# Letting ScalarE or VectorE take each cast and copy of the attention and folding stage, by the planner's estimates

## The chip, the cores and the metric

The kernel runs on one core of a Trainium2 chip. The engines named here are TensorE (PE, matrix products; PEld is its weight load), VectorE (DVE), ScalarE (ACT), GpSimd (POOL) and SyncE (SP), which only issues transfers. Each engine works through its own list in the order in which the instructions were recorded; an instruction whose input is not there holds up all that stand behind it in that list. The metric is the time of one execution in microseconds (us), the median over three runs.

## The reference

An attention over 4 batches x 12 heads, 448 tokens, head width 64, with soft-capped scores; then two feed-forward layers in a row.

```python
scores = cap * np.tanh(scale * q @ k.T / cap)
attn = np.exp(scores - max) / (sum + 1e-09)
x = attn @ v                       # 1792 x 768
x = ((x @ w1) * (x @ w2)) @ w3 @ w_out
h = x @ w_in
solu = h * softmax(h)
out = (layernorm(solu) * g_ln) @ w_out2
```

Between the product of the gates and `h` stand three matrices and no nonlinearity, so the kernel multiplies w3, w_out and w_in with each other first: these products of weights alone are the folds.

## The kernel before, in words

Every fp32 operand of a product is split into a high part, the operand cast to fp32r, and a low part, the operand less its high part; a product is then three matmuls (low by high, high by low, high by high). `cast` (L324) makes the high part on ACT, `low` (L327) the low part on DVE.

**The stages.** Stage one interleaves two streams on PE. One is attention: 24 pairs of heads, each with four blocks of scores (`scores`, L401, tiles `sc`, blocks 0 to 2 for two heads and block 3 for the rest of the keys of both), a tanh and an exp on ACT for each block (`exps`, L422: L426 and L431, tile `p`), and the product with the values and the sums (`values`, L480, tiles `o` and `n`, L486). The other, `beside` (L987), first folds w_out with w3 (`f1`, 576 matmuls, L658), then w_in with that (`f2`, 288 matmuls, L692), then begins the gated layer (`ab`, L935). When attention is done, stage two runs the rest of the gated layer, and stage three the last layers.

**Where the fold's operands come from.** A weight lands by DMA in one of three buffers `ld`, three DVE instructions turn it from 64-bit to 32-bit floats in one of two buffers `cv` (`convert`, L306: L314, L317, L320), then follow `cast` (L325) and `low` (L328). The operands are called `w_o` (w_out), `w_3` (w3), `w_i` (w_in), `wt` (the gates) and, loaded back from memory, `w34` (profile: w<-l). Attention's own are `qh`, `ql`, `kh`, `kl` from the loads `qd`, `kd` (`split_pair`, L375), and, for the gated layer, `xs` from `xr`.

**What sets the order.** Stage one is recorded by a planner, the class `Order` (L70). A step is a tuple: its engine, a rank, how long the engine is taken (`pitch`), when its result is there (`late`), and the instruction. `put` (L76) queues a step with the time at which its inputs are ready; `advance` (L103) takes, engine by engine, the step that can begin first by these estimates (then the lowest rank). The loop at L1073 decides for PE by the same clock: if the next piece of attention is ready it goes, otherwise one matmul of `beside` goes if its operands are ready, otherwise the clock moves on. So the estimates decide only the order; what happens on the chip is set by that order and the true durations. Before the change each step names one engine: casts and copies ACT, except the casts of pair 1 on DVE (L387; pair 0 is not split). After attention `order.live` is false, and steps are recorded at once in program order.

**Buffers that hold attention.** Scores use two places in PSUM, each taken from its first matmul until its exp has ended. Block 3 of a pair with an odd number therefore waits for the exp of block 2 of the pair before it.

Of the kernel before, what the change touches and what calls it, by code (L numbers as in the profile page):

```python
# [9 lines left out]
F32 = mybir.dt.float32  # L10
# [22 lines left out]
PLAIN, XR = 6, 5  # L33
# [36 lines left out]
class Order:  # L70
# [63 lines left out]
class Ahead:  # L134
# [20 lines left out]
    def step(self, n=1):  # L155

        for taken in range(n):
            if self.rest is not None:
                key, rest = self.rest
                for *_, do in rest():  # L160
                    do()
# [8 lines left out]
            for *_, do in first():  # L170
                do()
            self.rest = key, rest
            self.at += 1
            self.loads()
        return n
# [54 lines left out]
def attention_moe_solu(ctx: ExitStack, tc: tile.TileContext, q, k, v, cap, w12, w3t, wo, win, wout2, g_ln, out):  # L230
# [93 lines left out]
    def cast(th, x):  # L324
        act.copy(th, x)  # L325
# [8 lines left out]
    def plan64(key, src, n, dst, gate=None, there=None):  # L334

        i, slots, to = len(ahead.items), [], []

        def first():
            steps = convert(i, n, slots)
            return steps  # L340

        def begin():
            to.extend((*dst(), cvs.pop(i)))
            cast(to[0], to[2])

        def rest():
            return [("act", 1, 500, 680, begin), ("dve", 3, 610, 750, lambda: low(*to)), ("none", 0, 0, 0, lambda: ring["cv"].give(slots[0], order.now))]
# [27 lines left out]
    def split_pair(n, t):  # L375
# [5 lines left out]
        def make(name, w, x):  # L381
# [98 lines left out]
    def values(n):  # L480
# [21 lines left out]
        order.put(("act", 0, 460, 620, lambda: act.copy(to, out[:, :S])), order.now + 300, lambda t: ring["o"].give(slot, t))  # L502
        if n < PLAIN or m % 2 == 1:
# [22 lines left out]
            def keep():  # L526
# [3 lines left out]
                act.copy(copied[0], total[:, :S])  # L530
# [4 lines left out]
            order.put(("act", 0, 460, 620, keep), order.now + 300, kept)  # L535
# [80 lines left out]
    def load34(m):  # L616
# [12 lines left out]
        def high():  # L629
            t.append(ev_p.tile([P, 2, NC * P], F32R, tag="w34", bufs=2, name=f"w34_{f}_{nh}"))  # L630
            held_at["w34", m] = ring["w34"].take()
            cast(t[0][:, 0], ld[0])
# [6 lines left out]
        def landed(time):  # L639
            order.chain([("act", 1, 780, 920, high), ("dve", 1, 880, 1020, lambda: low(t[0][:, 0], t[0][:, 1], ld[0]))], time, finished, lambda: ring["w34"].when())  # L640
# [5 lines left out]
    def fold():  # L646
        for fq in range(NQ):
            for c in range(NC):
# [12 lines left out]
                def evict(f=f, fq=fq, c=c, slot=slot):  # L661
                    ev = []

                    def copy():
                        ev.append(ev_p.tile([P, HALF], F32, tag="ev", bufs=2, name=f"e1_{fq}_{c}"))
                        ev.append(ring["ev"].take())
                        act.copy(ev[0][:, :QW], f[:, :QW])
# [13 lines left out]
                    order.put(("act", 0, 310, 460, copy), order.now + 300, kept, lambda: ring["ev"].when())  # L681
                evict()
        for m_, (nh, f_) in enumerate(todo):
# [12 lines left out]
            def evict(f=f, f_=f_, nh=nh, slot=slot):  # L696
                ev = []

                def copy():
                    ev.append(ev_p.tile([P, HALF], F32, tag="ev", bufs=2, name=f"e2_{f_}_{nh}"))  # L700
                    ev.append(ring["ev"].take())
                    act.copy(ev[0], f)
# [4 lines left out]
                order.put(("act", 0, 510, 680, copy), order.now + 300, kept, lambda: ring["ev"].when())  # L707
# [52 lines left out]
    def plan_x(b, parts=range(NPAIR // 2)):  # L760
        for part in parts:
# [51 lines left out]
    def plan_sums(kind, dr, t_dr, i_, part, n):  # L813
# [12 lines left out]
        ahead.add((kind, i_, part), lambda: landing(i, four(dr, i_, part, n), 4 * n, F32), list, lambda: [(rest,)], None, lambda: 0.0 if "ts" in place else None)  # L826
# [26 lines left out]
    def plan_block(m, part):  # L853
        there = since((lambda: "ws" in place) if m != EARLY[4] else (lambda: (NF + 5, PASSES[1][1]) in fin and ("tg", NF // 2 - 1, 1) in ahead.done))
        ahead.add(("f", m, part), lambda: block_load(m, part, W4, tw_dr, fifth(m)), list,
                  lambda: [(lambda: block_split(ws[m], part),)], None, there)
# [62 lines left out]
    ahead.add("a0", load_first, list, lambda: [(first_operands,)], None, since(lambda: (NF + 2, PASSES[1][0]) in fin))  # L919

    def gated():
# [21 lines left out]
        def evict(f, b, i):  # L943
            bank_, slot = pp[f, b, i]

            def copy():
                pp["a", f, b] = place["ab"].tile([P, S], F32, tag="a", bufs=2, name=f"a_{f}_{b}")
                held_at["a", f, b] = ring["a"].take() if order.live else 0
                act.copy(pp["a", f, b], bank_[:, :S])  # L949
# [16 lines left out]
            if i == 0:  # L966
                order.put(("act", 0, 460, 620, copy), order.now + 300, lambda t: ring["f"].give(slot, t), lambda: ring["a"].when())
# [76 lines left out]
    with tc.manual_schedule():  # L1044
# [28 lines left out]
        for when, go in attend():  # L1073
            while True:
# [19 lines left out]
                assert waits[0] < 3e5, (order.now, pos, ask)  # L1094
# [348 lines left out]
```

## Time and profile before

| | us |
|---|---|
| median of three runs | 804.28 (803.32 to 804.76) |
| the profiled execution, its own time | 806.41 |
| its span in the trace | 804.6 |

Busy in the span: PE 785.3 us (98%), DVE 534.1 (66%), ACT 454.3 (56%), POOL 54.2 (7%). PE is the engine whose work cannot be taken away here, so its idle time and the time in which its clock is granted at half are what can be saved. Of the PE's time, matmuls at L935 take 233.8 us, at L486 78.6, at L658 76.3, at L692 68.3. The mean granted clock is 0.985 of full speed: it is 1.00 in most slices of the span and lower in the first eighth. The profile's rows read: line, engine, operation, out<-in, shape, count, then busy time and mean time of one, or in a view in order of time the start, the duration, and in brackets the idle time just before and what ended it.

### The profile page before, as it was taken

The numbers are of one execution on the slowest core, as the hardware profiler recorded it, in microseconds if no ns is written. First come the engines' busy times: TensorE is split into PE (matmuls) and PEld (weight loads), VectorE is DVE, ScalarE is ACT, GpSimd is POOL, SyncE is SP. The second block draws the span as 40 slices with busy tenths as digits, with TensorE's granted clock in tenths as the row PEclk, the third lists the DMA queues.
The fourth block names the chain that finished last, engine by engine and source line by source line (L and its number), as shares of the span: only waits on it lengthen the run. The fifth ranks groups of instructions, "written<-read, shape, count | busy, mean of one in ns | idle before, by whom it ended". The sixth has DMA issues, their size and how long they took to land.

```text
span 804.6 us, 11753 instructions
## 1 busy us (share of the span) xinstructions
PE 785.3 (98%) x4259; PEld 640.1 (80%) x4259; DVE 534.1 (66%) x938; ACT 454.3 (56%) x689; POOL 54.2 (7%) x106
## 2 busy tenths in 40 slices
PE   6989899999999999999999999999999999999998
PEld 3556668896776567766999999999788888899997
DVE  5466766678985356786678474332686668878972
ACT  5788766737868677766233221112476667845642
POOL 0101100100110011000000100000011111100000
PEclk8889999999999999999999999999999999999999
DMA  6475645487794349464898899982733335997431
GB/s 237 150 216 183 200 156 162 141 268 270 262 300 122 91 132 290 126 220 185 298 316 273 247 374 402 372 284 86 221 111 123 111 101 122 281 201 144 130 92 78
DMA packets 145705, 162.48 MB, mean 202 GB/s; under 512 B 66612, under 2 KB 116336, under 8 KB 144112
## 3 DMA queue, kind: packets, MB, share of 16 engines
q1 hardware_dynamic: 143056, 156.01, 60.6%
q0 software_dynamic: 2592, 5.73, 3.3%
q8 instruction: 33, 0.54, 0.3%
q14 instruction: 24, 0.20, 0.1%
HBM read 114.04 MB, written 47.53 MB: 201 GB/s over the span
## 4 chain that ended last, share of the span: by engine, by line
PE 89%; DMA 3%; ACT 3%; DVE 3%; issue 1%; SPq 0%; POOL 0%; DVEq 0%; ACTq 0%
PE ab L935 27%; PE u L1130 16%; PE f L658 9%; PE o L486 8%; PE f L692 8%; PE v L1130 8%; PE sc L413 6%; PE y L1130 4%; PE n L486 2%; PE sc L409 2%; ACT sc L426 1%; ACT p L431 1%; DMA wg<-wg_dr 1%; DMA rb<-r_dr 1%; DMA qd<-in_q 1%
## 5 line engine op out<-in xcount | busy, mean ns | idle before, releaser
L935 PE MATMUL ab<-xs,wt 128*128 128x448 f32 x1152 | 233.8, 363 | 0.0
L935 PEld LDWEIGHTS ab<-xs,wt 128*128 128x128 f32 x1152 | 215.5, 188 | 18.7 <-issue 4.5
L426 ACT ACTIVATE sc<-sc,small 128x896 f32<-128x896 f32 (+1 forms) x96 | 83.4, 892 | 51.5 <-PE sc L413 49.8
L431 ACT ACTIVATE p<-sc,small 128x896 f32<-128x896 f32 (+1 forms) x96 | 85.0, 921 | 0.4
L1130 PE MATMUL u<-ws,a 128*128 128x512 f32 x336 | 80.2, 390 | 0.3 <-DVE a L1258 0.3
L658 PEld LDWEIGHTS f<-w,w_o 128*128 128x128 f32 x576 | 72.8, 197 | 8.5 <-issue 4.1
L486 PE MATMUL o<-p,vd 128*64 128x448 f32 x384 | 78.6, 552 | 0.0
L658 PE MATMUL f<-w,w_o 128*128 128x256 f32 x576 | 76.3, 291 | 1.5 <-ACT w_o L325 0.6
L1130 PEld LDWEIGHTS u<-ws,a 128*128 128x128 f32 x336 | 63.0, 188 | 13.9 <-DVE a L1258 0.7
L692 PE MATMUL f<-w_i,w 128*128 128x512 f32 x288 | 68.3, 393 | 0.0
L692 PEld LDWEIGHTS f<-w_i,w 128*128 128x128 f32 x288 | 53.6, 188 | 13.9 <-issue 3.0
L1130 PE MATMUL u<-wg,a 128*128 128x384 f32 x336 | 62.1, 335 | 0.0
L486 PEld LDWEIGHTS o<-p,vd 128*64 128x64 f32 x384 | 25.7, 138 | 41.9 <-issue 41.9
L1130 PEld LDWEIGHTS u<-wg,a 128*128 128x128 f32 x336 | 58.6, 188 | 0.3 <-DVE a L1258 0.3
L949 ACT COPY a<-ab 128x448 f32<-128x448 f32 x32 | 16.9, 531 | 65.7 <-PE ab L935 57.8
L317 DVE SCALAR_TENSOR_TENSOR cv<-ld,cv 128x512 uint32<-128x512 uint32 (+1 forms) x80 | 51.5, 661 | 1.1
L320 DVE SCALAR_TENSOR_TENSOR cv<-ld,cv 128x512 uint32<-128x512 uint32 (+1 forms) x80 | 51.3, 660 | 0.8
L1254 ACT CAST a<-s 128x512 fp32r<-128x512 f32 (+1 forms) x42 | 31.3, 754 | 31.2 <-DVE s L1276 17.0
L314 DVE TENSOR_SCALAR cv<-ld 128x512 uint32<-128x512 uint32 (+1 forms) x80 | 32.0, 408 | 20.6 <-DMA ld<-in_w 8.3
L452 DVE TENSOR_TENSOR s<-p,p 128x896 f32<-128x896 f32 x18 | 19.7, 1092 | 34.0 <-ACT p L431 24.0
L1130 PE MATMUL v<-ws,a 128*128 128x512 f32 x168 | 40.4, 389 | 0.0
L1258 DVE TENSOR_TENSOR a<-s,a 128x512 fp32r<-128x512 f32 (+1 forms) x42 | 35.5, 851 | 5.8 <-ACT a L1254 5.8
(140 smaller groups left out, 1084.1 us busy)
## 6 DMA issues: line engine op xcount, KB each, us to landing
ld<-in_w SPq DMA_DIRECT2D x24, 512.0 KB, 5.0
w_dr<-wt SPq DMA_DIRECT2D x6, 1536.0 KB, 7.1
wt<-w_dr SPq DMA_DIRECT2D x6, 1536.0 KB, 8.6
ld<-in_w3t SPq DMA_DIRECT2D x16, 512.0 KB, 4.1
ab_dr<-abs SPq DMA_DIRECT2D x32, 224.0 KB, 4.1
ldx<-ab_dr SPq DMA_DIRECT2D x14, 512.0 KB, 4.4
c_dr<-h SPq DMA_DIRECT2D x14, 512.0 KB, 2.7
ldx<-c_dr SPq DMA_DIRECT2D x56, 128.0 KB, 3.3
```

Of the source, the lines that this page charges most:

```text
L314: dve.tensor_scalar(d[1], d[0][:, :, 1], 5, 2, ALU.logical_shift_left, ALU.logical_shift_right)
L317: dve.scalar_tensor_tensor(d[1], d[0][:, :, 1], 0xC0000000, d[1], ALU.bitwise_and, ALU.bitwise_or)
L320: dve.scalar_tensor_tensor(d[1], d[0][:, :, 0], 29, d[1], ALU.logical_shift_right, ALU.bitwise_or)
L413: pe.matmul(sc[:, j, :S], keys[rows], qq[rows, :], start=(m == 0), stop=(m == len(terms) - 1))
L426: act.activation(sc[:, :w, :S], sc[:, :w, :S], AF.Tanh, scale=qscale)
L431: act.activation(p, sc[:, :w, :S], AF.Exp, scale=capt)
L486: pe.matmul(dst[i * width:(i + 1) * width, :S], weights, moving, start=first, stop=stop)
L658: pe.matmul(f[:, :QW], lw[:, a], rw[:, e], start=(g == 0 and m == 0), stop=(g == NF - 1 and m == 2))
L692: pe.matmul(f, w34[m_][:, a, c, :], rw[:, e], start=(c == 0 and m == 0), stop=(c == NC - 1 and m == 2))
L935: pe.matmul(pp[f, b, i][0][:, :S], w[:, u], xs[b, c][:, e], start=begins, stop=(c == NC - 1 and m == 2))
L1130: pe.matmul(banks[g], a[r][m][:, p, k * P:(k + 1) * P], b[m][:, e, k, :], start=(first and k == 0 and i == 0), stop=(k == NF // 2 - 1 and ...
L1258: dve.tensor_tensor(lo, source(r, m), raw(hi), ALU.subtract)
```

## The change

A step may now name the engine "any" and give the estimates of both engines. When such a step is queued, `put` works out for each engine when it would be done: the latest of the engine's clock, the step's readiness and the present, plus the step's own pitch, plus the pitch of what waits there with the same or a better rank and is ready no later. DVE takes it if it would be done more than 1000 ns (`LEAN`) sooner than ACT; otherwise ACT does. Once attention is over, such steps go to ACT. The casts of pair 1 lose their fixed place on DVE, the order's estimates for these steps come from one formula, and the slot of a split weight is taken when its conversion begins, not at its cast.

```diff
-PLAIN, XR = 6, 5
+PLAIN, XR, LEAN = 6, 5, 1000.0
     def put(self, step, ready, then=None, when=None, loose=False):
         engine, rank, pitch, late, do = step
+        if engine == "any":
+            if self.live:
+                due = {e: max(self.clock[e], ready, self.now) + t[0] + sum(x[3] for x in self.waiting.get(e, ()) if x[0] <= rank and x[2] <= ready) for e, t in pitch.items()}
+                engine = "dve" if due["dve"] + LEAN < due["act"] else "act"
+                pitch, late = pitch[engine]
+            else:
+                engine = "act"
+            do_on, chosen = do, engine
+            do = lambda: do_on(chosen)
...
-    def cast(th, x):
-        act.copy(th, x)
+    def cast(th, x, engine="act"):
+        if engine == "act":
+            act.copy(th, x)
+        else:
+            dve.tensor_copy(th, x)
+
+    def copying(n, psum=False):
+        return {"act": (90 + 0.84 * n, 250 + 0.84 * n), "dve": (40 + 1.06 * n, 170 + 1.06 * n) if psum else (30 + 0.75 * n, 130 + 0.75 * n)}
...
         def first():
             steps = convert(i, n, slots)
-            return steps
+            def one(do=steps[0][4]):
+                to.extend(dst())
+                do()
+            return [(*steps[0][:4], one), *steps[1:]]
...
-            return [("act", 1, 500, 680, begin), ("dve", 3, 610, 750, lambda: low(*to)), ...
+            return [("any", 1, copying(n), None, begin), ("dve", 3, 610, 750, lambda: low(*to)), ...
...
-            if n < 2:
-                dve.tensor_copy(both[-2], x)
-            else:
-                cast(both[-2], x)
-        where = "dve" if n < 2 else "act"
-        steps = [(where, 1, 470, 640, lambda: make("q", S, qd)), (where, 1, 520, 690, lambda: make("k", HALF, kd)),
+            cast(both[-2], x, engine)
+        steps = [("any", 1, copying(S), None, lambda e: make("q", S, qd, e)), ("any", 1, copying(HALF), None, lambda e: make("k", HALF, kd, e)),
...
-            order.put(("act", 0, 460, 620, keep), order.now + 300, kept)
+            order.put(("any", 0, copying(S, True), None, keep), order.now + 300, kept)
...
-            order.chain([("act", 1, 780, 920, high), ("dve", 1, 880, 1020, ...
+            order.chain([("any", 1, copying(NC * P), None, high), ("dve", 1, 880, 1020, ...
...
-                    steps.append(("act", 1, 470, 640, lambda to=to, i=i: cast(to[:, 0], x[:, i])))
+                    steps.append(("any", 1, copying(S), None, lambda e, to=to, i=i: cast(to[:, 0], x[:, i], e)))
```

The other copies of stage one (`xr`, both folds' results `e1` and `e2`, and `a`) become "any" in the same way.

Net, 48 instructions go from ACT's list to DVE's: 32 casts of 128x512, 7 of 128x768 (`w34`), 8 of 128x448 (`xs`) and one copy of 128x256 out of PSUM. Since the planner's clock runs differently, the interleaving on PE changes too: before the values of pair 6, 231 fold matmuls stand where 175 stood; before those of pair 10, 633 against 620; at the end of attention, 1083 against 1113. The number of PE's instructions stays.

**Place one, the start, on DVE.** The first rows after the first conversions have begun, before and then with the change (line numbers shift by up to 16).

```order
L317 SCALAR_TENSOR_TENSOR cv0_163<-ld0_136,cv0_163 128x512
L384 CAST qh1_170<-qd1_143 128x448
L317 SCALAR_TENSOR_TENSOR cv1_165<-ld1_138,cv1_165 128x512
L384 CAST kh1_178<-kd1_142 128x512
L320 SCALAR_TENSOR_TENSOR cv0_163<-ld0_136,cv0_163 128x512
L328 TENSOR_TENSOR ql1_171<-qd1_143,qh1_170 128x448
L320 SCALAR_TENSOR_TENSOR cv1_165<-ld1_138,cv1_165 128x512
L328 TENSOR_TENSOR kl1_179<-kd1_142,kh1_178 128x512
```

With the change:

```order
L326 SCALAR_TENSOR_TENSOR cv0_164<-ld0_136,cv0_164 128x512
L326 SCALAR_TENSOR_TENSOR cv1_166<-ld1_138,cv1_166 128x512
L329 SCALAR_TENSOR_TENSOR cv0_164<-ld0_136,cv0_164 128x512
L329 SCALAR_TENSOR_TENSOR cv1_166<-ld1_138,cv1_166 128x512
L337 CAST w_o_0_0_163<-cv0_164 128x512
L344 TENSOR_TENSOR w_o_0_0_163<-cv0_164,w_o_0_0_163 128x512
L344 TENSOR_TENSOR ql1_178<-qd1_143,qh1_177 128x448
L344 TENSOR_TENSOR w_o_0_0_163<-cv1_166,w_o_0_0_163 128x512
L344 TENSOR_TENSOR kl1_186<-kd1_142,kh1_185 128x512
```

The two casts of pair 1 have left this list for ACT's, and its low parts now stand behind both conversions, a cast and two low parts of `w_o`.

**Place two, pair 3, on DVE.** From the low part of `w_3_0_3` to the next converted operands, before and then with the change.

```order
L328 TENSOR_TENSOR w_3_0_2_370<-cv4_300,w_3_0_2_370 128x512
L328 TENSOR_TENSOR w_3_0_3_372<-cv5_306,w_3_0_3_372 128x512
L314 TENSOR_SCALAR cv6_391<-ld6_239 128x512
L328 TENSOR_TENSOR ql3_367<-qd3_292,qh3_366 128x448
L314 TENSOR_SCALAR cv7_405<-ld7_357 128x512
L328 TENSOR_TENSOR kl3_383<-kd3_293,kh3_382 128x512
```

With the change:

```order
L337 CAST w_3_0_3_315<-cv5_316 128x512
L344 TENSOR_TENSOR w_3_0_3_315<-cv5_316,w_3_0_3_315 128x512
L337 CAST kh3_388<-kd3_309 128x512
L344 TENSOR_TENSOR ql3_385<-qd3_308,qh3_384 128x448
L344 TENSOR_TENSOR w_o_0_0_163<-cv6_322,w_o_0_0_163 128x512
L344 TENSOR_TENSOR kl3_389<-kd3_309,kh3_388 128x512
L323 TENSOR_SCALAR cv7_411<-ld7_258 128x512
L323 TENSOR_SCALAR cv8_425<-ld8_373 128x512
L326 SCALAR_TENSOR_TENSOR cv7_411<-ld7_258,cv7_411 128x512
L326 SCALAR_TENSOR_TENSOR cv8_425<-ld8_373,cv8_425 128x512
```

One conversion more (`cv6`) is done ahead of pair 3's low parts, and its operand's low part stands between them.

**Place three, pairs 6 and 7, on PE.** From the scores that need pair 7's first place to those that need its second, before and then with the change.

```order
L413 MATMUL sc6_2_978<-qh6_744,kh6_759 128x448 x2
L413 MATMUL sc7_0_985<-ql7_909,kh7_927 128x448 x2
L413 MATMUL sc7_0_985<-qh7_908,kl7_928 128x448 x2
L413 MATMUL sc7_0_985<-qh7_908,kh7_927 128x448 x2
L658 MATMUL f1_1_0_958<-w_3_1_1_914,w_o_0_0_188 128x256 x4
L409 MATMUL sc7_3_1017<-ql7_909,kh7_927 128x448
```

With the change:

```order
L429 MATMUL sc6_2_1040<-qh6_807,kh6_822 128x448 x2
L429 MATMUL sc7_0_1047<-ql7_986,kh7_989 128x448 x2
L429 MATMUL sc7_0_1047<-qh7_985,kl7_990 128x448 x2
L429 MATMUL sc7_0_1047<-qh7_985,kh7_989 128x448 x2
L674 MATMUL f1_1_1_1011<-w_3_1_2_882,w_o_1_1_410 128x256 x5
L674 MATMUL f1_1_1_1011<-w_3_1_3_913,w_o_1_1_410 128x256 x6
L674 MATMUL f1_1_2_1076<-w_3_1_0_769,w_o_1_1_410 128x256 x6
L674 MATMUL f1_1_2_1076<-w_3_1_1_826,w_o_1_1_410 128x256 x6
L674 MATMUL f1_1_2_1076<-w_3_1_2_882,w_o_1_1_410 128x256 x3
L425 MATMUL sc7_3_1107<-ql7_986,kh7_989 128x448
```

Where 4 fold matmuls stood between `sc7_0` and `sc7_3`, 26 stand now; at pair 3, 12 stand where none stood, and they need the operand made from `cv7`.

## Rows read from the trace of the kernel before

**Rows 1.** Busy time by stage: window, length, engines, PE's clock, DMA share, GB/s.

```profile
0.00:104.00 104.00, 90.84 (x542) 56.72 (x544) 64.17 (x119) 77.35 (x116) 10.85 (x24) 0.89 0.61 192
104.00:384.00 280.00, 278.78 (x1648) 203.32 (x1647) 193.53 (x305) 194.23 (x299) 23.64 (x46) 1.00 0.62 197
384.00:804.60 420.60, 415.64 (x2073) 380.06 (x2071) 276.45 (x516) 182.75 (x275) 19.74 (x37) 1.00 0.66 207
```

**Rows 2.** PE's waits: total us, times, longest.

```profile
PE sc L409 <- ACT p L431: 7.9, 6, 2.3
PE sc L413 <- ACT w_o L325: 2.9, 1, 2.9
```

**Rows 3.** The same from 104 to 384 us.

```profile
PE sc L409 <- ACT p L431: 1.2, 2, 0.7
```

**Rows 4.** PE's matmuls in order of time, 9 to 24 us.

```profile
15.56 0.74 PE L413 MATMUL sc<-qh,kl 64*128 64x448 f32 x2 [0.63 <-DVE kl L328]
...
18.73 0.74 PE L409 MATMUL sc<-ql,kh 128*128 128x448 f32 x1 [2.06 <-ACT p L431]
```

**Rows 5.** PE's matmuls in order of time, 41 to 130 us.

```profile
42.82 0.74 PE L409 MATMUL sc<-ql,kh 128*128 128x448 f32 x1 [2.27 <-ACT p L431]
...
44.23 3.23 PE L658 MATMUL f<-w,w_o 128*128 128x256 f32 x12
...
54.46 1.68 PE L658 MATMUL f<-w,w_o 128*128 128x256 f32 x12
...
71.72 0.50 PE L658 MATMUL f<-w,w_o 128*128 128x256 f32 x2 [0.63 <-ACT w_o L325]
72.44 1.70 PE L658 MATMUL f<-w,w_o 128*128 128x256 f32 x12 [0.23 <-DVE w_o L328]
...
96.22 0.47 PE L409 MATMUL sc<-ql,kh 128*128 128x448 f32 x1 [1.61 <-ACT p L431]
...
97.63 4.94 PE L658 MATMUL f<-w,w_o 128*128 128x256 f32 x19 [0.52 <-ACT w L325]
```

**Rows 6.** Busy time in four windows; columns as in rows 1.

```profile
15.20:25.40 10.20, 7.78 (x27) 3.79 (x29) 8.36 (x16) 9.60 (x14) 0.00 (x0) 0.50 0.80 276
42.50:49.30 6.80, 6.48 (x25) 5.28 (x27) 5.14 (x10) 5.32 (x10) 0.56 (x1) 0.50 0.82 259
97.00:104.00 7.00, 6.33 (x28) 5.58 (x29) 6.78 (x13) 4.03 (x9) 0.55 (x1) 0.51 0.50 164
168.00:232.00 64.00, 64.00 (x341) 49.77 (x341) 56.85 (x90) 42.27 (x68) 3.95 (x9) 1.00 0.84 279
```

**Rows 7.** ACT's groups by shape: busy us, mean ns; idle before.

```profile
L325 ACT CAST w<-l 128x768 fp32r<-128x768 f32 x16 | 13.4, 843 | 6.9 <-PE f L692 6.9
L325 ACT CAST w<-cv 128x512 fp32r<-128x512 f32 x16 | 9.9, 640 | 0.0
```

**Rows 8.** DVE's groups by shape.

```profile
L317 DVE SCALAR_TENSOR_TENSOR cv<-ld,cv 128x512 uint32<-128x512 uint32 x64 | 42.7, 687 | 0.8
L314 DVE TENSOR_SCALAR cv<-ld 128x512 uint32<-128x512 uint32 x64 | 26.4, 422 | 14.4 <-DMA ld<-in_w 8.3 <-DMA ld<-in_wo 5.7
L328 DVE TENSOR_TENSOR w<-cv,w 128x512 fp32r<-128x512 f32 x16 | 10.9, 689 | 21.0 <-ACT w L325 20.8
```

**Rows 9.** Line 384, casts on DVE: duration ns min/median/max, start.

```profile
L384 DVE CAST qh<-qd x1: 394/394/394, 11.8 to 11.8; 128x448 fp32r<-128x448 f32 x1
L384 DVE CAST kh<-kd x1: 421/421/421, 12.7 to 12.7; 128x512 fp32r<-128x512 f32 x1
```

**Rows 10.** DVE's waits: total us, times, longest.

```profile
DVE w L328 <- ACT w L325: 24.8, 12, 9.2
DVE w_o L328 <- ACT w_o L325: 14.7, 6, 4.4
```

**Rows 11.** ACT in order of time, 28 to 60 us.

```profile
33.39 1.91 ACT L431 ACTIVATE p<-sc,small 128x896 f32<-128x896 f32 x2
35.17 0.58 ACT L325 CAST qh<-qd 128x448 fp32r<-128x448 f32 x1
```

**Rows 12.** POOL's gather of sums, line 549: duration ns min/median/max.

```profile
L549 POOL DMA_DIRECT2D inv<-x x12: 636/658/881, 30.0 to 89.9; - x12
```

More of the change, by code (lines that the diff above doesn't have):

```diff
@@ L159, in step @@
                 key, rest = self.rest
-                for *_, do in rest():
-                    do()
+                for step in rest():
+                    self.order.put(step, 0.0)
                 self.done.add(key)
@@ L169, in step @@
                 return taken
-            for *_, do in first():
-                do()
+            for step in first():
+                self.order.put(step, 0.0)
             self.rest = key, rest
@@ L339, in first, with begin @@
             steps = convert(i, n, slots)
-            return steps
-        def begin():
-            to.extend((*dst(), cvs.pop(i)))
-            cast(to[0], to[2])
+            def one(do=steps[0][4]):
+                to.extend(dst())
+                do()
+            return [(*steps[0][:4], one), *steps[1:]]
+        def begin(engine):
+            to.append(cvs.pop(i))
+            cast(to[0], to[2], engine)
         def rest():
-            return [("act", 1, 500, 680, begin), ("dve", 3, 610, 750, lambda: low(*to)), ("none", 0, 0, 0, lambda: ring["cv"].give(slots[0], order.now))]
+            return [("any", 1, copying(n), None, begin), ("dve", 3, 610, 750, lambda: low(*to)), ("none", 0, 0, 0, lambda: ring["cv"].give(slots[0], order.now))]
         def open_():
@@ L501, in values @@
         to = xr[b, m // 2][:, m % 2]
-        order.put(("act", 0, 460, 620, lambda: act.copy(to, out[:, :S])), order.now + 300, lambda t: ring["o"].give(slot, t))
+        order.put(("any", 0, copying(S, True), None, lambda e: cast(to, out[:, :S], e)), order.now + 300, lambda t: ring["o"].give(slot, t))
         if n < PLAIN or m % 2 == 1:
@@ L529, in keep @@
                     copied[0] = copied[0][:, 0]
-                act.copy(copied[0], total[:, :S])
+                cast(copied[0], total[:, :S], engine)
             def kept(t):
@@ L680, in gone @@
                             saved[2 * fq] = saved[2 * fq + 1] = t
-                    order.put(("act", 0, 310, 460, copy), order.now + 300, kept, lambda: ring["ev"].when())
+                    order.put(("any", 0, copying(QW, True), None, copy), order.now + 300, kept, lambda: ring["ev"].when())
                 evict()
@@ L706, in kept @@
                     order.put(("sp", 0, 450, 5000, lambda: sync.dma_start(out=w_dr[f_, :, nh * HALF:(nh + 1) * HALF], in_=ev[0])), t, lambda t: ring["ev"].give(ev[1], t))
-                order.put(("act", 0, 510, 680, copy), order.now + 300, kept, lambda: ring["ev"].when())
+                order.put(("any", 0, copying(HALF, True), None, copy), order.now + 300, kept, lambda: ring["ev"].when())
             evict()
@@ L825, in rest @@
                 sync.dma_start(out=t_dr[2 * m:2 * m + 2, :, i_, part * n:(part + 1) * n].rearrange("t p n -> p t n"), in_=t[m])
-        ahead.add((kind, i_, part), lambda: landing(i, four(dr, i_, part, n), 4 * n, F32), list, lambda: [(rest,)], None, lambda: 0.0 if "ts" in place else None)
+        ahead.add((kind, i_, part), lambda: landing(i, four(dr, i_, part, n), 4 * n, F32), list, lambda: [("none", 0, 0, 0, rest)], None, lambda: 0.0 if "ts" in place else None)
     def rows(part):
@@ L918, in first_operands @@
         begin(6, s2)
-    ahead.add("a0", load_first, list, lambda: [(first_operands,)], None, since(lambda: (NF + 2, PASSES[1][0]) in fin))
+    ahead.add("a0", load_first, list, lambda: [("none", 0, 0, 0, first_operands)], None, since(lambda: (NF + 2, PASSES[1][0]) in fin))
     def gated():
@@ L966, in evict @@
             if i == 0:
-                order.put(("act", 0, 460, 620, copy), order.now + 300, lambda t: ring["f"].give(slot, t), lambda: ring["a"].when())
+                order.put(("any", 0, copying(S, True), None, copy), order.now + 300, lambda t: ring["f"].give(slot, t), lambda: ring["a"].when())
             else:
@@ L1093, in attention_moe_solu @@
                 waits[0] += 50.0
-                assert waits[0] < 3e5, (order.now, pos, ask)
+                assert waits[0] < 3e5
         ahead.over = xq.over = True
```

24 lines of the change are left out of this document (12 added, 12 removed).

## The prediction

> **What bounds the kernel now.** I read the busy times by stage first: PE is busy 278.8 of 280 us from 104 to 384 us and 415.6 of 420.6 after that, but 90.8 of 104 at the start, and there alone its granted clock is below 1.00, at 0.89 [rows 1]. PE's own matmuls are the same before and after, so a gain can only come out of the first 104 us: 13.2 us of idle time, a little of it before any data is there, and the clock. Then the waits: PE waited 7.9 us for an exp's end and 2.9 for pair 1's operands [rows 2]; 1.2 of the 7.9 lie after 104 us [rows 3], so stage one's long remainder has almost nothing to give. Then PE in order of time, for where the waits lie: four places. The first is the start [rows 4]. At 42.82 PE had waited 2.27 us, and twelve fold matmuls then took 3.23 us where twelve later ones take 1.68; at 71.72 and 72.44 it waited 0.63 and 0.23, without a loss of speed; at 96.22 and 97.63 it waited 1.61 and 0.52 [rows 5]. After the first, second and fourth the clock was granted at 0.50, that is 1.2 instead of 2.4 GHz, for 10.2, 6.8 and 7.0 us [rows 6]: there a busy us gives half. So a wait costs twice, and the fourth place costs 1.61 + 0.52 + 6.33 / 2 = 5.3 us, the second 2.27 + 6.48 / 2 = 5.5.
>
> Last the engines behind the waits. DVE's low parts waited 24.8 + 14.7 us for casts on ACT [rows 10], in ACT's list behind tanh and exp. That kept fold operands back, so that the planner had no matmuls to put between attention's scores where an exp was still running.
>
> **What the moves cost.** Off ACT go 32 casts at 0.64 us and 7 at 0.84 [rows 7], with nine smaller at less than 0.64: at most 32 us. On DVE a 128x512 cast took 0.42 us, one of 128x448 0.39 [rows 9]. 128x768 is not shown: between 0.42 and twice that, by width 0.63. The one copy out of PSUM is not shown either; I take 0.4, and even 0.69 [rows 8] would not matter once. DVE gets 32 x 0.42 + 8 x 0.39 + 7 x 0.63 + 0.4 = 21 us, over stage one's 384 us, where it is busy 64.2 + 193.5 [rows 1]. Neither engine is PE's limit in sum; what counts is the four places.
>
> **First place, the start.** ACT now does pair 1's q cast, which cannot begin before the load is there at 11.8 us [rows 9]; tanh, k cast, exp and the cast of `cv1` follow, five instructions of some 0.64, to 15.0. Behind that cast DVE has `cv1`'s low part and then pair 1's second one, 0.69 each [rows 8]: 16.3 us, where PE got it at 15.56 [rows 4]. This is a new wait of 0.7 us, and the conversions of `cv2` stand behind it on DVE. Then PE has six fold matmuls ahead of block 3 of pair 1. Their operand is ready after three conversions, a cast and a low part (0.42 + 0.69 + 0.69 + 0.42 + 0.69, somewhat less where they overlap) at about 19.0; at half clock they take 1.6 (half of 3.23), so block 3 starts at 20.6 instead of 18.73 [rows 4]: 1.9 late. Against that, the six are done (0.8 at full speed), and what ran at half clock until 25.4 [rows 6] begins later and so runs in part at full speed (1.0). Sum +0.1. Bounds: -1.0, if half of the 2.06 us wait for the exp goes, to +2.9, if nothing is given back and the 2.9 us wait grows by a third.
>
> **Second place, pair 3.** ACT still casts `qh3` after the exps that end at 35.3 [rows 11]; with a start some 1 us later it ends at 36.8. DVE, which has nothing else to do by its order, then runs the low part of q, that of `cv6` (its cast stands two behind `qh3` on ACT, so 37.9 + 0.7), that of k, twice the first conversion, twice the second and the third, the cast and the low part of `cv7`: 38.6 + 0.6 + 0.8 + 1.3 + 1.2 + 0.4 + 0.7 = 43.6 us. PE has by then done sums, block 3 of pair 2, 6 + 12 fold matmuls and two blocks of scores, at 42.5, and now has twelve more that need `cv7`: it waits 1.1 us. After them the exp is done and block 3 of pair 3 goes at once, but the next sixteen need `cv8`, which ACT casts only after another exp: 1.0 us more. So 2.1 us stay of 2.27. The fold matmuls in between split them, so the clock may stay up: waits of 1.61 and 0.52 us were followed by half clock, of 0.63 and 0.23 not, and 1.1 and 1.0 lie between. If it stays, -3.3; if it falls, -0.1; I take the middle, -1.7. Ends: -5.5, if both waits are hidden, to +2.
>
> **Third place.** The operands that came late at 71.7 are now cast on DVE itself, `cv13` and `cv15`, and only `cv14` waits for ACT; by the same addition the last is there about 1.5 us ahead of its matmuls. -0.9, or 0 if a load is late.
>
> **Fourth place, pair 7.** Four fold matmuls (4 x 0.14, from 1.68 for 12 [rows 5]) and 1.61 us of waiting made 2.2 us between `sc7_0` and the exp's end. Now 26 stand there: 3.6 us, 1.4 more than is needed. They must have their operands: by then DVE has made twenty conversions of 0.42 + 3 x 0.69 = 2.5 us, 13 casts, seven pairs of low parts (1.4) and some 4 us of sums, 69 us in all; begun at 9 and with some 6 us of waits it is through at 84, and PE asks for the last at about 88. So this wait and its clock go: -5.3; 0 if a new wait takes its place.
>
> **Later.** Up to 384 us the order is as before in kind, with somewhat fewer matmuls between attention's steps towards the end. Before, 280 us held 1.2 us of waits [rows 3]; I add as much again, +1.2 (0 to 5). The later end of stage one's fold work costs nothing: 30 gated matmuls move into stage two, where PE runs them at the same clock.
>
> **Sum:** 0.1 - 1.7 - 0.9 - 5.3 + 1.2 = -6.6. The profiled span of 804.6 would be 798.0, its own time 806.41 would be 799.8; the median of the runs, 804.28, lies 2.1 below that profiled time, and the same difference makes it 797.7.
>
> **A rule against it.** POOL issued its gathers of attention's sums in 0.64 to 0.88 us, beside 64 conversions of 0.42 us on DVE [rows 8, 12]. The Trainium skill's page "SBUF — State Buffer", section "SBUF: two separate sides", says that a DVE copy of fp32 within SBUF takes the port pair that GpSimd needs to write its DMA descriptors, so that such a DMA stands still meanwhile. By that rule each of the 47 new casts could hold up one issue. By the rows a hold-up so far is at most 0.88 - 0.64 = 0.24 us, and the gathers feed `xs`, which PE asks for much later; twelve of them make 2.9 us on POOL, none of it on PE.
>
> **The rivals.** *The waits come back elsewhere.* They end with an exp (7.9 of PE's waits [rows 2]), the estimates put an instruction's wait too low as before, and a place with little cover again lets the clock fall. For it: two such places in 104 us before. Against it: at pairs 5, 7, 9 and 11 the order now has 26 matmuls or more where the fourth place needed 16. One such place costs 5.4: 803. *VectorE becomes the late engine in the second fold, and the kernel slower.* From 168 to 232 us DVE is busy 56.9 of 64 [rows 6], and some 6 us of the moved casts fall there, five to seven of `w34` among them, which PE needs at once. If PE waits twice for them by 1.5 us and the clock falls each time (3.2 us, half of 6.48), that is 9.4 us: 797.7 + 9.4 = 807. It decides from about 8 us of such losses. Against it: the order takes DVE only where it would be done 1 us sooner, and DVE's own waits for ACT go. *POOL is held up* until `xs` is late: 21 gathers by 0.42 make 8.8 us at worst, 806; nothing in rows 2 shows a PE wait for it. *Better than forecast:* the clock stays up at the second place and no wait is added later: -9.4, 794.9. That the change does nothing is excluded by the order of the instructions.
>
> **Chances.** Forecast 0.50 (796 to 801), better 0.20, waits back 0.12, VectorE late 0.13, POOL 0.03, 0.02 for the rest. A measurement tells 0.2%, 1.6 us, from no change. Forecast, better, and a twentieth from where a rival takes only part of the gain make faster 0.75; most of the first rival is the same, 0.11; slower 0.14. Range: down to 793.5, the better case and a little of the start's gain; up to 804.6, which leaves out the slower cases.
>
> **What would show it.** In the profile after: no PE wait and clock 1.00 between 90 and 106 us (fourth place); fold matmuls waiting for `w_o`'s low part near 43 to 47 us (second), and whether the clock is 0.50 behind it; block 3 of pair 1 near 20.6 us; DVE's waits for casts down from 39.5 us to under 20, ACT some 30 us less busy in stage one and DVE 21 more. It would be wrong if PE waited for `w34` or `w_i` after 168 us, or if half clock were granted anywhere after 104 us.

## The result and the profile after

The changed kernel takes 793.84 us (median of 4 runs, 793.36 to 796.14), the kernel before beside it 804.52 (4 runs, 803.32 to 805.26): a ratio of 0.987, interval 0.985 to 0.990. That is 10.7 us faster, where 6.6 were forecast; the time lies in the range, 3.9 us below the forecast and next to the better case of the rivals, 794.9. The profiled execution took 793.63 us, its span is 791.9, its mean granted clock 0.995. One execution of the kernel with the choice up to 104 us, 1311.2 us at a mean clock of 0.60, is left out of that kernel's numbers below.

First the busy times of the stages of the changed kernel; columns as in rows 1.

```profile
0.00:104.00 104.00, 96.04 (x636) 62.24 (x637) 78.92 (x149) 75.61 (x110) 10.50 (x24) 0.97 0.68 222
104.00:384.00 280.00, 278.98 (x1615) 204.59 (x1614) 205.14 (x341) 176.79 (x263) 24.80 (x47) 1.00 0.63 203
384.00:791.90 407.90, 403.30 (x2011) 368.37 (x2010) 267.43 (x498) 178.72 (x268) 19.19 (x35) 1.00 0.66 203
```

Against [rows 1], the first 104 us hold 5.2 us more of PE's busy time and 94 more matmuls, at a clock of 0.97 instead of 0.89, and the next 280 us are unchanged. The last stretch runs at the same clock and is 12.7 us shorter, because it begins further on in the work.

The same for three pieces of the first 104 us, and below them the one stretch that is still at half clock.

```profile
0.00:26.00 26.00, 19.40 (x77) 11.09 (x78) 17.05 (x35) 16.86 (x24) 0.78 (x9) 0.87 0.74 257
26.00:60.00 34.00, 32.65 (x238) 18.70 (x236) 25.26 (x49) 26.36 (x40) 4.80 (x7) 1.00 0.69 212
60.00:104.00 44.00, 44.00 (x329) 32.44 (x326) 36.61 (x68) 32.39 (x49) 4.92 (x8) 1.00 0.65 209
...
15.30:22.10 6.80, 5.27 (x21) 3.16 (x17) 6.61 (x12) 4.24 (x6) 0.00 (x0) 0.50 0.64 206
```

Of the three stretches at 0.50 in [rows 6] (10.2, 6.8 and 7.0 us) one is left, of 6.8 us. From 60 to 104 us PE does not pause.

PE's waits in the changed kernel, whole span: what PE was about to do and what ended the wait; total us, times, longest.

```profile
PE sc L429 <- ACT w_o L335: 2.0, 1, 2.0
PE sc L425 <- ACT p L447: 1.4, 3, 0.7
PE f L674 <- DVE w L337: 1.4, 1, 1.4
PE sc L429 <- DVE kl L344: 0.9, 1, 0.9
PE f L674 <- ACT w_o L335: 0.5, 1, 0.5
PE f L674 <- DVE w_o L344: 0.4, 2, 0.2
```

The 7.9 us for an exp's end of [rows 2] are 1.4. Fold matmuls (`f`) now wait more for their operands than before (3.1 us in all against 1.3): 1.4 us at the start and a few tenths each later.

PE's matmuls of the changed kernel in order of time, the start first, then the second and the fourth place: start, duration, what, and in brackets the wait ahead of it.

```profile
13.63 0.47 PE L429 MATMUL sc<-ql,kh 64*128 64x448 f32 x2 [2.04 <-ACT w_o L335]
15.00 0.50 PE L429 MATMUL sc<-qh,kl 64*128 64x448 f32 x2 [0.91 <-DVE kl L344]
...
17.25 2.16 PE L674 MATMUL f<-w,w_o 128*128 128x256 f32 x6 [1.37 <-DVE w L337]
19.21 0.57 PE L425 MATMUL sc<-ql,kh 128*128 128x448 f32 x1
...
40.24 0.50 PE L674 MATMUL f<-w,w_o 128*128 128x256 f32 x2 [0.38 <-DVE w_o L337]
40.97 1.45 PE L674 MATMUL f<-w,w_o 128*128 128x256 f32 x10 [0.23 <-DVE w_o L344]
...
43.55 0.51 PE L674 MATMUL f<-w,w_o 128*128 128x256 f32 x2 [0.53 <-ACT w_o L335]
44.27 1.92 PE L674 MATMUL f<-w,w_o 128*128 128x256 f32 x14 [0.21 <-DVE w_o L344]
...
90.47 3.33 PE L674 MATMUL f<-w,w_o 128*128 128x256 f32 x26
93.64 0.36 PE L425 MATMUL sc<-ql,kh 128*128 128x448 f32 x1
```

At the second place one wait of 2.27 us [rows 5] has become four of 0.21 to 0.53, and the clock stays. At the fourth, 26 matmuls stand where four and a wait of 1.61 us stood, and there is none. At the start, where PE waited 2.06 us for an exp [rows 4], it now waits 1.37 us for an operand and then does six fold matmuls.

Last some of the 50 casts and copies now on DVE: count, duration in ns (min/median/max), first and last start, form.

```profile
L337 DVE CAST w<-cv x12: 380/420/428, 16.8 to 132.3; 128x512 fp32r<-128x512 f32 x12
L337 DVE CAST xs<-xr x8: 382/390/407, 173.5 to 311.0; 128x448 fp32r<-128x448 f32 x8
L337 DVE CAST w<-l x7: 549/553/560, 155.0 to 248.9; 128x768 fp32r<-128x768 f32 x7
L337 DVE COPY e<-f x1: 414/414/414, 92.6 to 92.6; 128x256 f32<-128x256 f32 x1
```

The prices of [rows 9] held in the whole stage; the two that no row showed are 0.55 us for 128x768 (0.63 was taken) and 0.41 for the copy out of PSUM (0.4).

### The profile page after: what moved, and what is told of

Read it like the earlier page. It is cut to its first block, busy times and chain, and to the rows that moved or that the text cites. A ratio compares the mean times of both kernels' runs of the same rounds, so it can differ in the third digit from the quotient of the medians.

```text
span 791.9 us, 11766 instructions
## 1 busy us (share of the span) xinstructions
PE 778.3 (98%) x4259; PEld 635.2 (80%) x4259; DVE 551.5 (70%) x986; ACT 431.1 (54%) x641; POOL 54.5 (7%) x106
## 4 chain that ended last, share of the span: by engine, by line
PE 91%; DMA 4%; DVE 2%; ACT 2%; issue 1%; SPq 1%; POOL 0%; DVEq 0%; ACTq 0%
PE ab L951 29%; PE u L1146 16%; PE o L502 9%; PE f L708 8%; PE v L1146 8%; PE f L674 7%; PE sc L429 6%; PE y L1146 4%; PE n L502 2%; PE sc L425 2%; DMA wg<-wg_dr 1%; DMA rb<-r_dr 1%; DMA qd<-in_q 1%; DMA w_dr<-e 1%; ACT p L447 1%
## 5 line engine op out<-in xcount | busy, mean ns | idle before, releaser
L674 PEld LDWEIGHTS f<-w,w_o 128*128 128x128 f32 x576 | 70.7, 191 | 10.6 <-issue 4.1
L674 PE MATMUL f<-w,w_o 128*128 128x256 f32 x576 | 74.4, 285 | 3.3 <-DVE w L337 1.4
L970 DVE TENSOR_TENSOR abs<-ab,a 128x448 f32<-128x448 f32 x32 | 19.8, 620 | 41.5 <-PE ab L951 23.8
```

What stands on the lines that cost most here:

```text
L674: pe.matmul(f[:, :QW], lw[:, a], rw[:, e], start=(g == 0 and m == 0), stop=(g == NF - 1 and m == 2))
```

## The experiments

The account to be tested has two parts. **Supply:** casts made on DVE in the first 104 us bring fold operands sooner, so that the planner has matmuls to put between the scores. **Clock:** what a wait costs is also the half clock behind it. Rivals: the relief of ScalarE over all of stage one is what counts, or the new estimates' order by itself, or one part (pair 1's casts on ACT). Each ratio is against the kernel before, run beside it on the same chip.

**The choice up to 104 us alone.** 19 of the 50 casts stay on DVE.

```diff
-            if self.live:
+            if self.live and self.now < 104000.0:
...
```

> The choice between ScalarE and VectorE is made only until the planner's clock reaches 104 us; later casts and copies all go to ScalarE. 19 of VectorE's 50 casts remain, all before the ninth pair; PE's order is that of the changed kernel up to there. Supply theory (the gain comes from the first fold's operands being ready sooner, which closes PE's waits and keeps its clock up in the first 104 us): the whole gain, 793 to 796 us. Load theory (the gain comes from taking work off ScalarE wherever it is): 17 of 48 moved casts, so a third of the 10.7 us, about 800.5 us.

800.21 us, 0.995 (0.993 to 0.997): about a third of the gain. The number is the one that the relief of ScalarE had asked for; the trace is not. PE's busy time from 0 to 104 us is 96.46 us, 96.04 after (at 0.95 and 0.97), and at the second and fourth places the clock stays at 1.00. A part is lost at the start, where half clock holds 9.55 us of work instead of 5.27 (half of the difference is 2.1 us); the rest is lost later. This kernel's stretch at half clock, its busy row of 104 to 384 us, and PE's waits after 104 us (the first two up to 384 us, the others after):

```profile
16.80:27.00 10.20, 9.55 (x31) 5.09 (x33) 9.36 (x18) 8.12 (x12) 0.00 (x0) 0.50 0.67 221
...
104.00:384.00 280.00, 276.62 (x1607) 201.51 (x1606) 187.91 (x299) 190.64 (x293) 23.75 (x46) 1.00 0.62 192
```

```profile
PE sc L430 <- ACT p L448: 1.5, 1, 1.5
PE f L709 <- DVE w_i L345: 1.2, 1, 1.2
...
PE ab L952 <- ACT a L336: 1.4, 1, 1.4
PE ab L952 <- ACT wt L336: 0.8, 1, 0.8
```

PE idles 3.4 us where 1.0 are idle after, and 2.2 more for `a` and `wt`: of the 8.5 us between the two profiled spans (800.4 and 791.9) some 4.7 are idle time of PE after 104 us. So the early moves pull work forward, and with the later casts left on ACT part of it is given back.

**The choice after 104 us alone.** 38 casts on DVE, pair 1's two as before the change.

```diff
-            if self.live:
+            if self.live and self.now >= 104000.0:
...
```

> The choice is made only from the planner's 104 us on; before that all is as before the change (pair 1's casts on VectorE, the rest on ScalarE). 38 casts on VectorE, 36 of them late; PE's order is that of the kernel before up to pair 6. Supply theory: no gain, 803 to 805.5 us, with PE's waits near 42, 71 and 96 us and half clock behind them as before. Load theory: three quarters of the gain, 796 to 797.5 us.

803.4 us, 1.000 (0.999 to 1.002). The first 104 us hold PE's busy time of before, with the waits at the second and fourth places (2.24 and 1.97 us) and a clock of 0.92, which was 0.89:

```profile
0.00:104.00 104.00, 90.91 (x550) 56.25 (x552) 63.78 (x118) 78.29 (x117) 10.87 (x24) 0.92 0.61 195
```

ACT has 17 us less to do between 104 and 384 us (176.99 against 194.23 [rows 1]) and the time stays: the relief of ScalarE after 104 us is by itself worth nothing.

**The new estimates alone,** every cast on the engine of before (pair 1's on DVE).

```diff
-            if self.live:
+            if False:
...
```

> Only the order's estimates are the changed kernel's (from the formula, for ScalarE); every cast and copy stays on the engine it had before. PE's fold counts are those of before up to pair 18. All theories but one: 803 to 805.5 us. Rival (the new estimates, closer to the true durations, are what helps): under 800 us.

804.31 us, 1.000 (0.998 to 1.002). Nothing, so the choice of engine is needed for the order to change.

**The order alone.** The planner chooses as after, and its order is kept, but every cast is issued to ACT.

```diff
-            do = lambda: do_on(chosen)
+            do = lambda: do_on("act")
```

> The planner chooses and orders as in the changed kernel, so PE's list is the same, but every cast and copy is carried out by ScalarE, at the place in its list that the plan's time gives. Order theory (the gain comes from PE's new interleaving alone, with more fold matmuls between the scores): 793 to 796 us. Supply theory: the operands come late, VectorE's low parts wait for ScalarE again, and PE waits in front of fold matmuls that the new order puts early: most of the gain is lost, 799 to 806 us, with at least one stretch of half clock more than in the changed kernel.

798.38 us, 0.994 (0.992 to 0.996): about half of the gain, with every one of these casts on ACT. The row from 0 to 104 us and the largest waits of this kernel:

```profile
0.00:104.00 104.00, 95.24 (x622) 61.19 (x623) 70.31 (x127) 83.43 (x128) 10.95 (x24) 0.97 0.68 217
```

```profile
PE sc L425 <- ACT p L447: 2.9, 5, 0.8
PE sc L429 <- DVE ql L344: 1.8, 1, 1.8
PE f L674 <- ACT w L335: 1.8, 1, 1.8
PE f L674 <- ACT w_o L335: 1.4, 2, 1.0
```

The order fills PE (95.24 of 96.04) and keeps the clock as well as the whole change does. What the engine itself adds shows behind it: with ACT holding all casts, the waits of PE for ACT are back in small pieces, and from 104 to 384 us PE idles 3.0 us where 1.0 are idle after.

**Pair 1's casts back on DVE,** the rest as after.

```diff
-        steps = [("any", 1, copying(S), None, lambda e: make("q", S, qd, e)), ...
+        where = "dve" if n < 2 else "any"
+        steps = [(where, 1, 470, 640, q_) if n < 2 else ("any", 1, copying(S), None, q_), ...
```

> Pair 1's two casts stay on VectorE as before, everything else is chosen as in the changed kernel; PE's order is the changed kernel's. If the start's gain over the kernel before (about 2 us between 11 and 26 us in the trace) comes from pair 1's casts on ScalarE: 795.5 to 797 us, and pair 1's second score product starts near 15.5 us or later. If it comes from the fold matmuls that stand ahead of block 3 and bring the clock back sooner: 793.5 to 794.5 us, full clock from about 22 us on.

794.12 us, 0.990 (0.986 to 0.994), clock 0.87 in the first 26 us as after. What the start gained does not come from these two casts.

**The margin at 0 and at 2000 ns,** with 119 and 10 casts on DVE.

```diff
-PLAIN, XR, LEAN = 6, 5, 1000.0
+PLAIN, XR, LEAN = 6, 5, 0.0
```

> LEAN 0 instead of 1000 ns: a cast goes to whichever engine would be done first, 119 casts on VectorE instead of 50; by pair 6 PE has 162 fold matmuls behind it where the changed kernel has 231 and the kernel before 175. Load theory: VectorE takes a cast in 0.42 us where ScalarE takes 0.64, so more moved is better: 790 to 793 us. Supply theory: VectorE also makes the fold's operands, and casts of attention in its list push these back; less fold work between the scores, waits return: 796 to 802 us.

> LEAN 2000 ns: 10 casts on VectorE instead of 50, pair 1's casts on ScalarE; fold matmuls by pairs 2, 4, 6, 8: 79, 150, 246, 353, even more than in the changed kernel (64, 149, 231, 329). Supply theory: the order has the cover and the few casts that were latest have moved: 793 to 797 us. Load theory: a fifth of the gain, 802 to 803 us.

801.0 us, 0.997 (0.995 to 0.998), and 800.35 us, 0.996 (0.994 to 0.998). With margin 0 there is a place like the old fourth one again. PE's matmuls of that kernel near 92 us:

```profile
92.10 0.47 PE L425 MATMUL sc<-ql,kh 128*128 128x448 f32 x1 [2.28 <-ACT p L447]
94.40 0.74 PE L429 MATMUL sc<-ql,kh 64*128 64x448 f32 x2 [0.53 <-ACT p L447]
```

The scores at 94.40 take 0.74 us where they take 0.47 at full speed. This is the first rival of the prediction, waits that come back elsewhere, met in a neighbour of the kernel. With margin 2000 the waits for ACT's casts stay (2.5 us for pair 1's `ql`, 1.6 for `w_o`, 1.5 for `wt`). More casts on DVE is not better; as these traces read, what counts is which matmuls are ready at each exp.

**The start filled.** The changed kernel with nine and seven more matmuls on zeros, whose result nothing reads, around pair 1's first scores.

```diff
                     scores(*run[0], one)
+                    if run == ((0, 2), (1, 0)):
+                        for i in range(9):
+                            pe.matmul(idle[:, :S], zero[:, 0, :P], zero[:, 0], start=True, stop=True)
                     scores(*run[1], two)
...
+                    if run == ((0, 2), (1, 0)):
+                        for i in range(7):
+                            pe.matmul(idle[:, :S], zero[:, 0, :P], zero[:, 0], start=True, stop=True)
```

> The changed kernel with 9 matmuls on zeros in front of pair 1's first scores and 7 behind them, where PE waits 2.0, 0.9 and 1.4 us for operands; they add no work that anything waits for. Clock theory (a wait at the start costs twice, since the half clock behind it lasts from 15.6 to 22 us): the clock stays at 1.00 there, PE's 4.9 busy us at half become 2.4, less what then waits for exps: 1.0 to 2.4 us faster than the changed kernel, 791.5 to 793 us. Rival (the exps of pairs 0 and 1 set the pace at the start, PE's speed does not): no change, 793.5 to 794.5 us, or slower by up to 1 us if the added matmuls hold up the scores behind them.

791.65 us (791.23 to 792.43), 0.985 (0.982 to 0.988), 2.2 us less than the changed kernel and the fastest of all. The first stage:

```profile
0.00:104.00 104.00, 98.66 (x665) 65.00 (x665) 79.42 (x149) 75.60 (x110) 10.66 (x24) 1.00 0.68 223
```

The clock is 1.00 throughout. The stretch at 0.50 held 5.27 us of work, so at most 2.6 were to be had.

**The kernel before with its waits filled,** to price the clock by itself: matmuls whose result nothing reads, no operand sooner, no order changed.

```diff
+FILL = {2: 10, 6: 7}
...
+                    def last(x=n + phase, one=one):
+                        if x in FILL:
+                            spare = ps.tile([P, HALF], F32, tag="o", bufs=2, name=f"spare{x}")
+                            for i in range(FILL[x]):
+                                pe.matmul(spare[:, :S], ready[x][2][:, :P], ready[x][0], start=True, stop=True)
+                        scores(x, 3, one)
```

> The kernel before, its order of work untouched, with added matmuls whose result nothing reads: ten (128x448) in the 2.27 us wait ahead of block 3 of pair 2 and seven in the 1.61 us wait ahead of block 3 of pair 6. No operand comes sooner and no wait gets shorter. Clock theory (what a wait costs is mostly the half clock behind it, 6.48 / 2 and 6.33 / 2 us): clock 1.00 from 26 to 104 us and 804.0 - 6.4 = 797.6. Rival (the waits themselves and the late operands are the cost, the clock only shows them): 803 to 804.5.

> As the one before, and with nine and seven matmuls on zeros around pair 1's first scores as in the changed kernel's filled start. Clock theory: the half clock of 15.2 to 25.4 us goes as well, at most 10.2 / 2 = 5.1 us, some 4: 793 to 794.5, that is, the change's whole gain without the change; what then stays between this and the filled changed kernel (791.7) is what shorter waits are worth by themselves, 1.5 to 3 us. Rival: 801 or more.

807.84 us, 1.006 (1.003 to 1.009), and 805.08 us, 1.004 (1.002 to 1.007): both slower. The matmuls stood in the wrong place. PE's matmuls of the first of the two near the second place:

```profile
35.52 2.30 PE L1046 MATMUL spare<-qh,kh 128*128 128x448 f32 x10
...
43.54 0.48 PE L410 MATMUL sc<-ql,kh 128*128 128x448 f32 x1 [2.29 <-ACT p L432]
...
44.94 3.23 PE L659 MATMUL f<-w,w_o 128*128 128x256 f32 x12 [0.52 <-ACT w_o L326]
```

Block 3 of pair 2 does not wait; that of pair 3 does. So 17 matmuls were added to a busy PE (2.30 us here, 1.68 at 88 us, and the time rose by 4.0), and the wait behind them is 2.29 us as it was 2.27 [rows 5]: it counts from PE's own scores, through tanh and exp, and no work ahead of the scores shortens it. Since no wait was filled at these two places, the kernels decide nothing on the clock there. The start's fill, which the second has as well (with the edit shown for the start), is worth 2.76 us between the two. The same kernel as the second, with the matmuls in the waits:

```diff
-FILL = {2: 10, 6: 7}
+FILL = {3: 9, 7: 6}
```

> The last two kernels had their added matmuls one pair too early (they ran at 35.8 and 88.2 us, where PE did not wait, and the waits of 2.29 and 1.61 us with the half clock stayed behind them). Here they stand in the waits themselves: nine ahead of block 3 of pair 3, six ahead of block 3 of pair 7, and the filled start as in the kernel with all three. The kernel before otherwise, no wait made shorter. Clock theory: half clock goes at all three places, 6.4 us at the second and fourth and, from the 2.76 us by which the start's fill moved the last pair of runs, 2.8 at the start: 804 - 9.2 = 794.8, and what remains to the filled changed kernel (791.7) is what shorter waits are worth alone. Rival (waits and late operands are the cost): 801, the start's 2.8 at most.

798.41 us (797.55 to 799.59), 0.994 (0.992 to 0.997): between the two theories' 794.8 and 801. The stage, the two places, and PE's waits for operands in this kernel:

```profile
0.00:104.00 104.00, 97.12 (x632) 61.68 (x632) 69.16 (x127) 81.80 (x123) 10.86 (x24) 1.00 0.67 211
```

```profile
36.78 2.09 PE L1052 MATMUL spare<-qh,kh 128*128 128x448 f32 x9
39.10 0.47 PE L410 MATMUL sc<-ql,kh 128*128 128x448 f32 x1 [0.23 <-ACT p L432]
...
40.51 0.50 PE L659 MATMUL f<-w,w_o 128*128 128x256 f32 x2 [0.53 <-ACT w_o L326]
41.23 1.41 PE L659 MATMUL f<-w,w_o 128*128 128x256 f32 x10 [0.23 <-DVE w_o L329]
```

```profile
PE f L659 <- ACT w_o L326: 1.2, 2, 0.6
PE f L659 <- ACT w L326: 0.5, 1, 0.5
PE f L659 <- DVE w_o L329: 0.4, 2, 0.2
PE f L659 <- DVE w L329: 0.3, 1, 0.3
```

The clock is 1.00 and 5.1 us are gained, not 9.2. Part of what the clock gives is lost again: the matmuls behind the filled waits are through sooner and then wait for their operands, 2.4 us in these four rows where the kernel before had 1.3. Another part is smaller in most runs of that kernel: 6.4 of the 9.2 was worked out from a profiled execution of before with a clock of 0.985, and between the two profiled executions the gain is 7.3 us (806.41 - 799.12). Against the changed kernel with its start filled, where the clock is 1.00 as well, 6.8 us remain (798.41 - 791.65; 7.3 if each is taken against its own runs of the kernel before): that is what the change is worth without the clock, work done in the waits.

A second reading of the clock's price needs no edit. Of the kernel before's 24 runs beside the filled changed kernel, the two at a mean clock of 0.996 took 800.05 and 800.16 us and the eleven at 0.989 took 803.02 to 804.52: some 3.7 us for 0.007 in one and the same program, nearly the clock that the change gains. What made these runs differ is not shown, and it can have made waits shorter too.

**The choice up to 250 us.** 38 casts on DVE; the last twelve of the changed kernel's are ACT's again. The time is the planner's own.

```diff
-            if self.live:
+            if self.live and self.now < 250000.0:
```

> The changed kernel with the choice until 250 us of the planner's time, ScalarE after. If the late moves are worth something at the second fold's operands (the one wait of 1.2 us near 172 us): 799. If they are worth something because the order behind them shifts as a whole: 793.5 to 796. If all of the late worth lies in the gated stage's copies after 290 us: 800.

795.14 us (793.65 to 796.99), 0.991 (0.988 to 0.995), the profiled span 791.9 as after. From 104 to 600 us PE waits as little as after:

```profile
PE f L709 <- DVE w_i L345: 0.6, 1, 0.6
PE u L1147 <- DVE a L1275: 0.3, 1, 0.3
PE sc L426 <- ACT p L448: 0.3, 1, 0.3
```

This kernel and the one that stops at 104 us lie 5.1 us apart; among their runs with a clock of 0.995 or more, which leaves most of the difference at the start out, it is 3.9 (794.6 and 798.5 in the mean). So some 4 us belong to the casts of 104 to 250 us. With them the waits near 300, 427 and 460 us go too, though the casts there are ACT's in both: the order behind shifts as a whole. The casts moved after 250 us are worth 1.3 us or nothing, within the two kernels' intervals.

## Why the prediction was right, and where its sizes were off

*What bounds the kernel* held: nearly all of the gain comes out of the first 104 us, the choice there is necessary (804.31 and 803.4 without it), and of the four places three kept their clock or lost their wait, while the start kept part of both. The rest of stage one had nothing to give, but it could take: without the moves between 104 and 250 us it takes some 4 us back.

By the trace, each term is PE's idle time that went and half of the busy time that is no longer at half clock. For the first, the row of the kernel before from 0 to 26 us, columns as in rows 1:

```profile
0.00:26.00 26.00, 18.24 (x63) 10.13 (x65) 14.60 (x30) 17.51 (x24) 0.78 (x9) 0.80 0.69 239
```

- Start, forecast +0.1: idle 26 - 18.24 against 26 - 19.40, -1.2, and (7.78 - 5.27) / 2 = -1.3 of clock: -2.4. Block 3 of pair 1 was forecast for 20.6 and stood at 19.21: the operand of the six fold matmuls was there at 17.25, not 19.0. Part of it is the load of pair 1, which ended at 10.97 instead of 11.8 us, and part is that ACT's five instructions overlapped: they took 2.65 us and not 3.2. In the kernel with the choice to 250 us PE's wait there is 2.9 us as before and block 3 stands at 19.87, still sooner than forecast; its time is nearly that of the changed kernel, so the load is not what makes the gain.
- Second place, forecast -1.7: four waits, 1.35 us in all, against 2.27, -0.9, and the clock stayed, -3.2: -4.2. The forecast stood in the middle of -3.3 and -0.1 (by its own terms -3.4 and -0.2), an average of two outcomes of which one happens; its waits of 1.1 and 1.0 us came out at 0.61 and 0.74, for `cv7`'s and `cv8`'s operands as named.
- Third place, -0.9: as forecast.
- Fourth place, -5.3: as forecast, 26 matmuls in 3.33 us, no wait, clock 1.00.
- Later, forecast +1.2: 1.0 us of waits instead of 1.2 up to 384 us, 4.6 instead of 5.0 after, -0.6.

They add up to about -13.4, the span fell by 12.7; by the medians the gain is 10.7, because the profiled execution of before lay 1.9 us above the median of its four runs (804.52) and that of after 0.2 below its own. For the profiled execution 799.8 was forecast and 793.63 measured, 6.2 less; that the median missed by 3.9 only is luck, since the last step took the same 2.1 us between profile and median for both kernels. The step that failed is the size of the first and second terms and of the later waits: the prediction charged 1.9 us for block 3 of pair 1 coming later, 2.1 for waits at the second place and 1.2 for waits after 104 us, 5.2 together; measured were 0.5 (19.21 against 18.73), 1.35 and -0.6, 1.3 together. A further 1.6 us is the second place's clock, which was counted half and came whole.

One price in it was too high all the same, and the sum did not show it: "a wait costs twice". Half of the work done at half clock is the most that it costs. Filling the waits of the kernel before at all three places gave 5.1 us where the half clock alone was priced at 9.2: in part because PE at full speed overtakes the casts, in part because the profiled execution of before had more half clock than most. The gain of 10.7 is then 3 to 4 us of clock (3.7 by the runs of before, 5.1 less the 2.2 that the changed kernel still leaves at its start) and some 7 of work done in the waits (6.8), where the prediction had 5.8 us of clock (3.2, 1.6 and 1.0) in a forecast of 6.6. Between the two profiles themselves the clock's share is larger: for the same 4259 matmuls PE's busy time fell by 6.9 us (785.3 to 778.3) and its idle time by 5.8; the profile of before had a clock of 0.985, 17 of the 24 runs above 0.987 to 0.989.

Of the rivals, the one called better than forecast came: the clock stayed up at the second place, no wait was added later, and its 794.9 is nearer to 793.84 than the forecast is. None of the slower ones came: after 168 us PE waits for neither `w34` nor `w_i`, though DVE was at 58.48 of 64 there:

```profile
168.00:232.00 64.00, 64.00 (x313) 46.13 (x311) 58.48 (x95) 39.62 (x59) 5.31 (x11) 1.00 0.84 270
```

Nor was POOL held up. Its gathers of the changed kernel, against [rows 12]:

```profile
L565 POOL DMA_DIRECT2D inv<-x x12: 636/637/843, 28.7 to 87.5; - x12
```

The median went from 658 to 637 ns and the longest from 881 to 843, with 50 casts and copies on DVE in stage one where two were. The rule of the Trainium skill's page "SBUF — State Buffer", section "SBUF: two separate sides", that a DVE copy of fp32 holds up GpSimd's descriptor writes, is not seen in these rows, but they hardly test it: only the first of the twelve gathers (28.65 us) had one of the new casts beside it (`kh`, 28.80), and it took 0.84 us, as the first one of the kernel before did with DVE idle beside it.

DVE's waits for casts, 39.5 us before [rows 10], are 3.3 for `w` and 1.9 for `w_o`; those of `ql` for `qh`, still cast on ACT, rose from 1.6 to 10.8. Over the span ACT is 23.2 us less busy and DVE 17.3 more, where some 30 and 21 were forecast.

What stays open is when the clock comes back at the start: at 22.1 us in the profile of the changed kernel, at 27.0 in that of the choice to 104 us, where the same matmuls stand. The load's end differs from run to run, and no kernel held it fixed.

## What to carry to other kernels

Where an engine-bound stage has waits, ask which work could stand in them and what keeps its operands back; moving a producer off the busy queue in front of it is worth what the planner can then put there, and here half of that came from the order alone. Price half clock from both sides: half of the stretch at most, and less by what the engine will overtake. A move that pulls work forward needs the stage behind it to keep up, or part of the gain goes back there: try the edit cut off at a stage's end before calling the later half of it useless.

## What the runs showed of the hardware

- Matmuls on zeros, whose result nothing reads, were enough to keep the granted clock up: with 16 of them the first 26 us went from 0.87 to 1.00, and the kernel from 793.84 to 791.65 us.
- Four waits of 0.21 to 0.53 us, between 39.9 and 44.3 us, left the clock at 1.00; one of 2.29 us was followed by half clock, twelve fold matmuls taking 3.23 us, although ten matmuls had been added before the scores ahead of it.
- One program's mean granted clock differs between executions: 24 runs of the kernel before had 0.984 to 0.996 and took 807.22 to 800.05 us, so a single profiled execution can lie some us off the median.
- A cast on DVE is not proportional in width: 420 ns for 512 columns, 553 for 768, 390 for 448.
